# Spreading w_out's block sums, two banks for the last pass, and copies ahead of activations in a feed-forward kernel

## The chip, the cores and the metric

One core of a Trainium2 chip runs the whole program. The metric is device time in microseconds for one execution, and lower is better. TensorE does the matmuls; VectorE and ScalarE read its banks, split numbers into a high and a low part and do the elementwise work; GpSimd (POOL) scales attention operands; SyncE (SP) issues nearly all transfers.

## The reference

Linear attention with a decay for each head (4 sequences, 8 heads, 768 positions of 64) gives x, which goes through a feed-forward layer:

```
attn_out = _attn_ref(q, k, v, lam)                 # 4 x 8 x 768 x 64
x = attn_out.transpose(0, 2, 1, 3).reshape(3072, 512)
h = x @ w_in                                       # 3072 x 2048
r = np.maximum(h, 0.0)
out = (r * r) @ w_out                              # 3072 x 512
```

All of it is in fp32. The matmuls take each factor as a high part and a low part and add three products: high by high, high by low, low by high.

## The kernel before, in words

The 3072 tokens are six slices (m = 0 to 5) of 512 tokens, that is, of four chunks of 128. The hidden features are 16 blocks of 128 (f = 0 to 15), or 8 pairs.

Slices 0 and 1 go straight: for each f, 12 matmuls of 128x512 for `x @ w_in`, then relu and square, then `project`, 12 matmuls into four accumulator banks. The other four are done two and two by a block scheme with 7 products where 8 would be needed. The loop over `pair(0, i, ...)` makes the hidden features of slices 2 and 3: for each pair of f, 7 products of 6 matmuls (`product`, banks X, Y, Z), joined by VectorE's adds into `temp`, and beside it the projection of slice 2 and the attention of slices 4 and 5. Then the fourth slice (m2 = 3) is projected: `again` casts the kept features `r` to a high part `gh` on ScalarE and a low part `gl` on VectorE, two buffers each, and `project` follows one step behind. Between these steps stand sums and parts of x (`x_sums`, `x_parts`) for the last two slices. The loop over `NPAIR` at line 1305 is the last w_in phase: the 7 products of each pair for slices 4 and 5, features kept in `k1`, `k2`, `l1`, `l2`, on which `kept` does relu and square in place. Its last pair begins to prepare the w_out stage (`prepare`: a cast to the high part on ScalarE, a subtraction for the low part on VectorE). Last comes `whole(0)` and `whole(1)`: the same scheme for `@ w_out`, seven passes of 48 matmuls of 128x256 for each of the two slices, on banks X, Y and Z.

Four of those passes need w_out's blocks added and subtracted. For each of the 8 units u (the blocks u and u + 8), `t_sums` does two adds and four subtractions on VectorE and a cast on ScalarE, `t_parts` the low part on VectorE, and `t_store` sends both parts to DRAM, from where `t_fetch` brings them into a ring of slots in the last stage. Units 0 to 5 (`SUMMED`) are done in the first six pairs of slices 2 and 3, units 6 and 7 in steps 2, 4 and 8, 10 of the fourth slice's projection.

Every engine runs its instructions in the order in which the program writes them; nothing reorders them. SyncE's transfers too wait in their order. A weight of the pairs is fetched 8 products ahead (`RING`), at the end of a product.

Of the kernel before, what the change touches and what calls it, by code (L numbers as in the profile page):

```python
# [7 lines left out]
F32 = mybir.dt.float32  # L8
F32R = mybir.dt.float32r
# [3 lines left out]
ALU = mybir.AluOpType  # L13
PSUM = bass.MemoryType.PSUM

P = 128
# [6 lines left out]
DM = H * D  # L23
# [3 lines left out]
G = 4  # L27
# [8 lines left out]
NPAIR = NF // 2  # L36
RING = 8
EARLY = 2 * NF - 3
SUMMED = 6
SUMS = (1, 2, 3, 5, 6, 7, 9, 11)  # L40
HALF = DM // 2

# [2 lines left out]
def body(ctx: ExitStack, tc: tile.TileContext, qT, kT, kvq, lam, w, out):  # L45
    nc = tc.nc
# [3 lines left out]
    wk = ctx.enter_context(tc.tile_pool(name="wk", bufs=2))  # L50
# [5 lines left out]
    V = nc.vector  # L56
# [156 lines left out]
    raw, cv, hole, beside, third = {}, {}, None, [], []  # L213
# [100 lines left out]
    Z = T - 1  # L314
# [8 lines left out]
    x = ZP  # L323
# [12 lines left out]
    for k in range(4):  # L336
# [394 lines left out]

    T1, T3, T4, T2 = range(4)

    def t_sums(u, sums):
        x = sums[:, 0]
        for k in range(2):
            j = w_out(u + k * NPAIR)
            add(
                x[:, 2 * k : 2 * k + 2].rearrange("p a n -> p (a n)"),
                wh[:, j].bitcast(F32), wl[:, j].bitcast(F32),  # L740
            )
        b11, b12, b21, b22 = (x[:, k] for k in range(4))
        sub(b11, b12, b11)
        sub(b12, b22, b12)
        sub(b22, b22, b11)
        sub(b21, b21, b22)
        nc.scalar.copy(sums[:, 1].bitcast(F32R), x)

    def t_parts(sums):
        x = sums[:, 0]  # L750
        V.tensor_tensor(out=x.bitcast(F32R), in0=x, in1=sums[:, 1], op=ALU.subtract)

    def t_store(u, sums):
        for k in range(2):
            nc.sync.dma_start(out=td[u, :, :, k], in_=sums[:, 1 - k])
# [75 lines left out]
    def kept(r):  # L831
        nc.scalar.activation(r, r, AF.Relu)
        nc.scalar.activation(r, r, AF.Square)
# [263 lines left out]
    for i in range(NPAIR):  # L1097
        t = (PLAIN + 2) * G + i

        def attention(first, then):  # L1100
            more = i + 1 < NPAIR
            x = burst(t + 1, True, more, first)
            then()
            keep(t, x)
            if i < SUMMED:
                t_parts(sums)
            if more:
                masked(t + 1)
                state(t + 1)
                prep_q(t + 1)  # L1110
                copy_vx(t + 1)
                copy_qx(t + 1)
            if i + 2 < NPAIR:
                load_kq(t + 2)
                load_v(t + 2)
                prep_k(t + 2)

        def between():
            nonlocal sums
            project(*p)  # L1120
            if i == 0:
                sums = wk.tile([P, 2, 4, HALF], F32, name="sums", tag="raw")
            if i < SUMMED:
                t_sums(i, sums)

        p = prev
        pair(0, i, temp, between, attention)
        if i < SUMMED:
            t_store(i, sums)
        prev = (m1, 2 * i + 1)  # L1130
    sums = sets[0].bitcast(F32).rearrange("p (k a n) -> p k a n", k=2, a=4)
    again(m2, 0)
# [1 line left out]
    for f in range(NF):  # L1134
        if f + 1 < NF:
            again(m2, f + 1)
        if f % 2 and f < 14:
            x_sums(f // 2)
            x_parts(f // 2)
        if f in (2, 8):  # L1140
            t_sums(SUMMED + f // 6, sums)
        if f in (4, 10):
            t_parts(sums)
            t_store(SUMMED + f // 6, sums)
        if f + 1 < NF:
            project(m2, f)
    prev = (m2, NF - 1)
# [87 lines left out]
    def multiply(n, j, bank, i, begin, end):  # L1235
        s_, p, k = n // 14, n // 2 % 7, n % 2
        w_, _ = factor(p, s_, k * G + j)
        at = j % 2 * HALF + i * C
        h, l = (part(n, e)[:, j // 2, at : at + C] for e in range(2))
        o = bank[:, i * HALF : (i + 1) * HALF]  # L1240
        for q, (x, y) in enumerate(((h, 0), (h, 1), (l, 0))):
            nc.tensor.matmul(  # L1242
                o, x, w_[:, y], start=begin and i == 0 and q == 0, stop=end and q == 2,
                skip_group_check=True,
            )

# [9 lines left out]
    def whole(s_):  # L1256
        p1, u2, u3, c11 = (temp[:, k] for k in range(4))
        banks_ = {}
        for p in range(7):
            if p in (0, 1, 4):  # L1260
                banks_["XY..Z"[p]] = ps_acc.tile([P, DM], F32, name="acc")
            bank = banks_["XYXYZYZ"[p]]
            begin, last = p in (0, 1, 4), p == 6 and s_ == 1
            for k in range(2):
                n = s_ * 14 + p * 2 + k
                prepare(n + LEAD)
                if last:
                    continue
                for j in range(G):
                    for i in range(2):  # L1270
                        multiply(n, j, bank, i, begin and k == 0 and j == 0, k == 1 and j == G - 1)
                    e = factor(p, s_, k * G + j)[1]
                    if e is not None:
                        t_fetch(e + len(t_ring))
            if p == 0:
                nc.scalar.copy(p1, bank)
            elif p == 1:
                nc.scalar.copy(u2, bank)
            elif p == 2:
                nc.scalar.copy(c11, bank)  # L1280
                send(s_, 0, 0, c11)
            elif p == 3:
                add(u3, bank, p1)
                sub(u2, u3, u2)
            elif p == 4:
                add(u3, bank, u3)
                send(s_, 1, 1, u3)
            elif p == 5:
                add(p1, bank, p1)
                send(s_, 1, 0, p1)  # L1290
            elif not last:
                add(u2, bank, u2)
                send(s_, 0, 1, u2)
            else:
                for i in range(2):
                    for k in range(2):
                        for j in range(G):
                            multiply(s_ * 14 + p * 2 + k, j, bank, i, False, k == 1 and j == G - 1)
                    cs = slice(i * HALF, (i + 1) * HALF)
                    add(u2[:, cs], bank[:, cs], u2[:, cs])  # L1300
                    t = (PLAIN + 3) * G + i
                    nc.sync.dma_start(out=out[t * C : (t + 1) * C, HALF:DM], in_=u2[:, cs])

    place = [r_of[k] for k in range(G)]
    for i in range(NPAIR):
        n = (NPAIR + i) * 7
        f1, f2 = 2 * i, 2 * i + 1
        p1, u2, u3, _ = (temp[:, k] for k in range(4))
        k1, k2 = (g_place(0, f) for f in (f1, f2))
        l1, l2 = (g_place(1, f) for f in (f1, f2))  # L1310
        X = ps_h.tile([P, N], F32, name="h")
        product(n, X, True)
        nc.scalar.copy(p1, X)
        Y = ps_h.tile([P, N], F32, name="h")
        product(n + 1, Y, True)
        add(u2, Y, p1)
        if i == NPAIR - 1:
            prepare(0)
        if i in range(1, 5):
            for s_ in range(2):  # L1320
                x = g_kept[s_][(i - 1) // 2][0][:, (i - 1) % 2 * 2 : (i - 1) % 2 * 2 + 2]
                sub(x[:, :, HALF:DM], x[:, :, 0:HALF], x[:, :, HALF:DM])
        product(n + 2, X, False)
        nc.scalar.activation(X, X, AF.Relu)
        nc.scalar.activation(k1, X, AF.Square)
        product(n + 3, Y, False)
        if i == 0:
            project(*prev, place=place)
        add(u3, Y, p1)
        Z = ps_acc.tile([P, N], F32, name="acc")  # L1330
        product(n + 4, Z, True)
        add(l2, Z, u3)
        product(n + 5, Y, False)
        add(k2, Y, p1)
        kept(l2)
        if i == NPAIR - 1:
            prepare(1)
        product(n + 6, Z, False)
        add(l1, Z, u2)
        kept(k2)  # L1340
        kept(l1)
    for n in range(2, LEAD):
        prepare(n)
    for n in range(len(t_ring)):
# [56 lines left out]
```

## Time and profile before

| | us |
|---|---|
| median of three runs | 584.71 |
| lowest, highest | 584.45, 585.79 |
| the profiled execution, its own time | 585.68 |
| its span, first to last instruction | 583.9 |
| TensorE busy with matmuls | 569.7 (98%) |
| TensorE busy with weight loads | 477.2 (82%) |
| VectorE busy | 390.0 (67%) |
| ScalarE busy | 337.1 (58%) |
| GpSimd busy | 84.4 (14%) |

A matmul's time in a row includes its latency, and rows of neighbours overlap, so "busy 98%" says that TensorE is rarely empty, not that it is never held up. Where it is held up shows in what the weight loads (PEld) and the matmuls (PE) waited for, and in the distance from one matmul's start to the next. The stages follow each other in time: opening and slices 0 and 1 until 232 us, the pairs of slices 2 and 3 until 371, the projection of the fourth slice until 419, the last w_in phase until 499, the w_out stage until the end.

### The profile page before, as it was taken

Reading aid. Unit: us, or ns where it says so; the run is one execution under the profiler, and the core shown is the slowest. Engines: PE = TensorE matmul, PEld = TensorE weight load, DVE = VectorE, ACT = ScalarE, POOL = GpSimd, SP = SyncE. Lnnn points to the kernel's source line nnn. Section 1 sums busy time; section 2 is a strip of 40 time slices with the busy share of each in tenths; the row PEclk is TensorE's granted clock in tenths of the full one; section 3 lists DMA queues with packets and bytes.
Section 4 is the critical chain, followed back from the end, with each engine's and each line's share of the span. In section 5 each row is a group of like instructions: output and inputs, shape, how many; then the busy total and the mean of one; then the engine's idle time right before and its main releaser. Section 6 shows DMA issues by size and latency. Waiting matters only on the chain.

```text
span 583.9 us, 13621 instructions
## 1 busy us (share of the span) xinstructions
PE 569.7 (98%) x5519; PEld 477.2 (82%) x5519; DVE 390.0 (67%) x687; ACT 337.1 (58%) x597; POOL 84.4 (14%) x96
## 2 busy tenths in 40 slices
PE   7899999999999999899999999998999999999997
PEld 5777888888888888788888888876878787999997
DVE  5899999936868676665677643467544434786771
ACT  3799989845656655555655545544356565643440
POOL 6512422332223100011111111000000000000000
PEclk7799999999999999999999999999999999999999
DMA  8668667145998853778666773321277664899431
GB/s 317 215 238 279 223 218 239 45 149 200 322 345 299 309 177 104 235 235 267 201 204 203 261 238 107 127 73 36 62 225 186 196 188 121 289 342 359 143 112 54
DMA packets 70270, 118.85 MB, mean 204 GB/s; under 512 B 5952, under 2 KB 31040, under 8 KB 70208
## 3 DMA queue, kind: packets, MB, share of 16 engines
q1 hardware_dynamic: 70208, 117.99, 61.2%
q8 instruction: 43, 0.70, 0.5%
q14 instruction: 19, 0.16, 0.1%
HBM read 88.60 MB, written 29.36 MB: 202 GB/s over the span
## 4 chain that ended last, share of the span: by engine, by line
PE 92%; DVE 3%; DMA 2%; issue 1%; ACT 1%; SPq 0%; POOL 0%; DVEq 0%; POOLq 0%
PE h L805 22%; PE h L637 15%; PE acc L1242 14%; PE acc L673 10%; PE acc L678 9%; PE acc L674 9%; PE h L433 4%; PE acc L805 4%; PE b L433 2%; PE att L433 2%; DMA set<-in_kvq 1%; DVE set L347 1%; DMA set<-in_w 1%; PE open L433 1%; DVE sums L347 1%
## 5 line engine op out<-in xcount | busy, mean ns | idle before, releaser
L673 PE MATMUL acc<-w,gh 128*128 128x512 f32 x224 | 89.7, 400 | 1.8 <-ACT gh L837 1.8
L678 PE MATMUL acc<-w,gl 128*128 128x512 f32 x224 | 87.7, 391 | 0.2 <-DVE gl L658 0.2
L674 PE MATMUL acc<-w,gh 128*128 128x512 f32 x224 | 87.5, 391 | 0.0
L805 PE MATMUL h<-w,ring 128*128 128x512 f32 x288 | 70.5, 393 | 1.6 <-DVE r L347 1.6
L805 PEld LDWEIGHTS h<-w,ring 128*128 128x128 f32 x288 | 53.4, 188 | 14.9 <-DVE r L347 2.3
L658 DVE TENSOR_TENSOR gl<-h,gh 128x512 fp32r<-128x512 f32 x40 | 27.5, 688 | 53.6 <-ACT h L653 53.6
L1242 PE MATMUL acc<-w 128*128 128x256 f32 x492 | 60.9, 283 | 0.5 <-DVE temp L347 0.5
L1242 PEld LDWEIGHTS acc<-w 128*128 128x128 f32 x492 | 59.9, 192 | 0.8 <-DVE temp L347 0.7
L637 PE MATMUL h<-xh,w 128*128 128x512 f32 x240 | 60.1, 392 | 0.0
L644 ACT ACTIVATE h<-h 128x512 f32<-128x512 f32 x40 | 23.3, 583 | 60.7 <-PE h L637 44.0
L347 DVE TENSOR_TENSOR temp<-h,temp 128x512 f32<-128x512 f32 x40 | 27.5, 689 | 41.8 <-PE h L805 33.1
L637 PEld LDWEIGHTS h<-xh,w 128*128 128x128 f32 x240 | 44.7, 188 | 10.0 <-DVE w L295 0.4
L673 PEld LDWEIGHTS acc<-w,gh 128*128 128x128 f32 x224 | 42.0, 188 | 12.4 <-ACT gh L837 3.1
L505 POOL TENSOR_TENSOR qs<-set,qpow 128x512 f32<-128x512 f32 (+1 forms) x21 | 26.4, 1255 | 174.5 <-PE b L433 172.9
L678 PEld LDWEIGHTS acc<-w,gl 128*128 128x128 f32 x224 | 42.0, 188 | 10.3 <-DVE gl L658 1.4
L674 PEld LDWEIGHTS acc<-w,gh 128*128 128x128 f32 x224 | 42.1, 188 | 8.6 <-POOL w L298 0.4
L805 PE MATMUL h<-w,wz 128*128 128x512 f32 x144 | 35.8, 393 | 0.0
L805 PE MATMUL h<-w 128*128 128x512 f32 x144 | 35.7, 392 | 0.0
L1220 DVE TENSOR_TENSOR w<-kept,w 128x1024 fp32r<-128x1024 f32 (+2 forms) x32 | 25.2, 820 | 10.9 <-ACT w L1219 10.9
L637 PE MATMUL h<-xl,w 128*128 128x512 f32 x120 | 32.2, 390 | 0.1
L1219 ACT CAST w<-kept 128x1024 fp32r<-128x1024 f32 (+2 forms) x32 | 22.6, 727 | 16.5 <-PE acc L1242 15.8
L805 PEld LDWEIGHTS h<-w,wz 128*128 128x128 f32 x144 | 26.7, 188 | 6.5 <-ACT temp L848 0.3
(240 smaller groups left out, 1168.6 us busy)
## 6 DMA issues: line engine op xcount, KB each, us to landing
ring<-wd SPq DMA_DIRECT2D x56, 256.0 KB, 3.1
raw<-in_w SPq DMA_DIRECT2D x22, 512.0 KB, 5.0
w<-td SPq DMA_DIRECT2D x42, 256.0 KB, 5.3
set<-in_kvq SPq DMA_DIRECT2D x16, 512.0 KB, 3.9
wd<-hl SPq DMA_DIRECT2D x16, 512.0 KB, 5.0
w<-wd SPq DMA_DIRECT2D x28, 256.0 KB, 3.0
wz<-wd SPq DMA_DIRECT2D x28, 256.0 KB, 2.9
td<-sums SPq DMA_DIRECT2D x12, 512.0 KB, 5.4
```

Source lines behind the costliest of these rows:

```text
L347: lambda o, x, y, op=op: V.tensor_tensor(out=o, in0=x, in1=y, op=op)
L433: nc.tensor.matmul(self.banks[row][rows[col], at : at + D], lhsT, rhs, start=key not in self.begun, stop=stop, skip_group_check=True,)
L505: nc.gpsimd.tensor_tensor(out=z, in0=x, in1=w_, op=ALU.mult)
L637: nc.tensor.matmul(h, wt[:, w_in(f), kt * P : (kt + 1) * P], x[:, kt], start=k == 0, stop=k == 11)
L644: nc.scalar.activation(h, h, AF.Relu)
L658: V.tensor_tensor(out=gl, in0=r, in1=gh.bitcast(F32), op=ALU.subtract)
L673: nc.tensor.matmul(accs[m][i], gh[:, cs], wh[:, j], start=f == 0, stop=False)
L674: nc.tensor.matmul(accs[m][i], gh[:, cs], wl[:, j], start=False, stop=False)
L678: nc.tensor.matmul(accs[m][i], gl[:, cs], wh[:, j], start=False, stop=end)
L805: nc.tensor.matmul(bank, w[:, kw * HALF + kt * P : kw * HALF + (kt + 1) * P], x_slot(2 * c + kt, kx), start=first and q == 0, stop=q == 5, ...
L1220: V.tensor_tensor(out=l, in0=x, in1=h.bitcast(F32), op=ALU.subtract)
L1242: nc.tensor.matmul(o, x, w_[:, y], start=begin and i == 0 and q == 0, stop=end and q == 2, skip_group_check=True,)
```

## The change

- `t_sums` is cut in three: `t_whole` (the two adds), `t_sums` (the four subtractions, or some of them) and `t_high` (the cast). `t_parts` is now `t_low`.
- The first pair of slices 2 and 3 carries no sums. The next five pairs carry units 0 to 4.
- Units 5 and 6 stand in the fourth slice's projection: adds at steps 0 and 6, subtractions at 2 and at 8 and 10, casts at 3 and 11, low parts and stores at 4 and 12.
- Unit 7 stands in the first three pairs of the last w_in phase.
- There, `kept(k2)` and `kept(l1)` move from a pair's end to the next pair, behind the copy of its first bank X.
- In the second slice of the last stage, bank Z's two halves of 256 columns lie in two banks (Z and z) in passes 4 and 6; the add of pass 4 is done half by half.

```
-SUMMED = 6
+SUMMED = 5
...
-            if i < SUMMED:
-                t_sums(i, sums)
+            if 0 < i <= SUMMED:
+                t_whole(i - 1, sums)
+                t_sums(sums)
+                t_high(sums)
...
-        if f in (2, 8):
-            t_sums(SUMMED + f // 6, sums)
-        if f in (4, 10):
-            t_parts(sums)
-            t_store(SUMMED + f // 6, sums)
+        if f in (0, 6):
+            t_whole(SUMMED + f // 6, sums)
+        if f in (2, 8, 10):
+            t_sums(sums, {2: (0, 1, 2, 3), 8: (0, 1), 10: (2, 3)}[f])
+        if f in (3, 11):
+            t_high(sums)
+        if f in (4, 12):
+            t_low(sums)
+            t_store(SUMMED + f // 12, sums)
...
-                o, x, w_[:, y], start=begin and i == 0 and q == 0, stop=end and q == 2,
+                o, x, w_[:, y], start=begin and q == 0, stop=end and q == 2,
...
+            if p == 4 and s_ == 1:
+                banks_["z"] = ps_acc.tile([P, DM], F32, name="acc")
             bank = banks_["XYXYZYZ"[p]]
+            pair_ = (bank, banks_["z"]) if "z" in banks_ and bank is banks_["Z"] else (bank, bank)
...
-                    add(u2[:, cs], bank[:, cs], u2[:, cs])
+                    add(u2[:, cs], pair_[i][:, cs], u2[:, cs])
...
         nc.scalar.copy(p1, X)
+        for x in remaining:
+            kept(x)
+        if i == 2:
+            t_high(sums)
         Y = ps_h.tile([P, N], F32, name="h")
         product(n + 1, Y, True)
         add(u2, Y, p1)
+        if i == 0:
+            t_whole(U, sums)
         if i == NPAIR - 1:
             prepare(0)
...
         add(l2, Z, u3)
+        kept(l2)
         product(n + 5, Y, False)
         add(k2, Y, p1)
-        kept(l2)
         if i == NPAIR - 1:
             prepare(1)
         product(n + 6, Z, False)
         add(l1, Z, u2)
-        kept(k2)
-        kept(l1)
+        if i < 2:
+            t_sums(sums, (2 * i, 2 * i + 1))
+        elif i == 2:
+            t_low(sums)
+            t_store(U, sums)
+        remaining = [k2, l1]
+    for x in remaining:
+        kept(x)
```

VectorE in the first pair of slices 2 and 3, before (`o` are the drain copies of slice 1, `r` the add that frees bank Z):

```order
L347 TENSOR_TENSOR temp<-h,temp 128x512
L682 COPY o<-acc 128x512 x2
L347 TENSOR_TENSOR sums<-w 128x512 x2
L347 TENSOR_TENSOR sums<-sums 128x256 x4
L347 TENSOR_TENSOR r<-h,temp 128x512
```

The same place after:

```order
L347 TENSOR_TENSOR temp<-h,temp 128x512
L682 COPY o<-acc 128x512 x2
L347 TENSOR_TENSOR r<-h,temp 128x512
L347 TENSOR_TENSOR temp<-h,temp 128x512
L347 TENSOR_TENSOR r<-h,temp 128x512
```

The six instructions of the sums are gone from between the drain copies and the adds.

ScalarE in the fourth slice's projection, before, from step 8's sums on (`set_94` holds the sums, `gh` are the high parts, `w<-held` the casts of x's sums):

```order
L747 CAST set_94<-set_94 128x1024
L837 CAST gh<-r 128x512
L780 CAST w<-held_1638 128x512 x2
L837 CAST gh<-r 128x512 x2
L780 CAST w<-held_1638 128x512 x2
L837 CAST gh<-r 128x512 x2
```

The same place after:

```order
L840 CAST gh<-r 128x512 x2
L783 CAST w<-held_1638 128x512 x2
L840 CAST gh<-r 128x512 x2
L783 CAST w<-held_1638 128x512 x2
L750 CAST set_94<-set_94 128x1024
L840 CAST gh<-r 128x512 x2
```

The cast of the sums has moved behind the next two pairs of casts of x's sums, that of step 11, and stands ahead of the high part that `again(m2, 13)` casts.

ScalarE at the start of the last pair of the last w_in phase, before (`temp<-h` is the copy of bank X, `w<-set_94` the cast of the w_out stage):

```order
L832 ACTIVATE kept<-kept 128x512
L833 ACTIVATE kept<-kept 128x512
L832 ACTIVATE kept<-kept 128x512
L833 ACTIVATE kept<-kept 128x512
L1313 COPY temp<-h 128x512
L1219 CAST w<-set_94 128x2x512
L1324 ACTIVATE h<-h 128x512
```

The same place after:

```order
L1337 COPY temp<-h 128x512
L835 ACTIVATE kept<-kept 128x512
L836 ACTIVATE kept<-kept 128x512
L835 ACTIVATE kept<-kept 128x512
L836 ACTIVATE kept<-kept 128x512
L1228 CAST w<-set_94 128x2x512
L1354 ACTIVATE h<-h 128x512
```

The four activations have moved from ahead of the copy to between the copy and the cast. VectorE's order is the same there before and after: the add to `temp`, the cast's low part (`w<-set_94,w`), the next add to `temp`.

## Rows read from the trace of the kernel before

**Rows 1.** The page's slices of the span: granted clock of TensorE, in tenths

```profile
PEclk7799999999999999999999999999999999999999
```

**Rows 2.** What weight loads waited for: us in total, times, longest

```profile
PEld acc L673 <- ACT gh L837: 3.1, 3, 1.7
...
PEld h L805 <- ACT temp L1313: 2.0, 7, 0.3
...
PEld acc L678 <- DVE gl L658: 1.4, 3, 0.6
```

**Rows 3.** Order of time, first pair: start, us, engine, line, operation [idle before]

```profile
240.55 2.88 PE L805 MATMUL h<-w,ring 128*128 128x512 f32 x12
...
241.36 1.28 DVE L347 TENSOR_TENSOR sums<-w 128x512 f32<-128x512 f32 x2
...
242.56 1.79 DVE L347 TENSOR_TENSOR sums<-sums 128x256 f32<-128x256 f32 x4
...
245.01 1.66 PE L805 MATMUL h<-w,ring 128*128 128x512 f32 x6 [1.58 <-DVE r L347]
```

**Rows 4.** Fourth slice's fifteen projections: window, us, busy by engine, clock, DMA share, GB/s

```profile
374.15:418.73 44.58, 42.58 (x182) 33.25 (x180) 31.67 (x48) 18.33 (x32) 0.00 (x0) 1.00 0.19 68
```

**Rows 5.** Order of time, VectorE and ScalarE, around unit 6's sums

```profile
382.04 1.79 DVE L347 TENSOR_TENSOR set<-set 128x256 f32<-128x256 f32 x4
...
383.87 1.05 ACT L747 CAST set<-set 128x1024 fp32r<-128x1024 f32 x1 [3.68 <-DVE set L347]
384.82 0.61 ACT L837 CAST gh<-set 128x512 fp32r<-128x512 f32 x1
...
385.47 0.69 DVE L658 TENSOR_TENSOR gl<-set,gh 128x512 fp32r<-128x512 f32 x1 [1.63 <-ACT gh L837]
```

**Rows 6.** Order of time there: the low part, then a step with sums of x

```profile
387.88 1.22 DVE L751 TENSOR_TENSOR set<-set 128x1024 fp32r<-128x1024 f32 x1
...
394.05 0.62 ACT L837 CAST gh<-r 128x512 fp32r<-128x512 f32 x1 [2.10 <-PE acc L674]
...
397.61 0.62 ACT L837 CAST gh<-r 128x512 fp32r<-128x512 f32 x1
```

**Rows 7.** Order of time, start of the third pair of the last w_in phase

```profile
440.97 2.88 PE L805 MATMUL h<-w,ring 128*128 128x512 f32 x12
...
442.56 0.63 ACT L833 ACTIVATE set<-set 128x512 f32<-128x512 f32 x1
443.09 0.57 ACT L1313 COPY temp<-h 128x512 f32<-128x512 f32 x1
...
443.71 3.03 PE L805 MATMUL h<-w 128*128 128x512 f32 x12
444.30 0.69 DVE L347 TENSOR_TENSOR temp<-h,temp 128x512 f32<-128x512 f32 x1 [2.44 <-PE h L805]
```

**Rows 8.** Order of time, last pair of that phase: cast, low part, next add

```profile
492.00 1.05 ACT L1219 CAST w<-set 128x1024 fp32r<-128x1024 f32 x1
...
493.08 1.23 DVE L1220 TENSOR_TENSOR w<-set,w 128x1024 fp32r<-128x1024 f32 x1
...
495.21 0.69 DVE L347 TENSOR_TENSOR temp<-h,temp 128x512 f32<-128x512 f32 x1 [0.91 <-PE h L805]
```

**Rows 9.** Order of time, the last pass, its two halves

```profile
573.95 2.32 PE L1242 MATMUL acc<-w 128*128 128x256 f32 x18
...
577.03 0.42 DVE L347 TENSOR_TENSOR temp<-acc,temp 128x256 f32<-128x256 f32 x1 [2.18 <-PE acc L1242]
...
577.51 2.42 PE L1242 MATMUL acc<-w 128*128 128x256 f32 x18 [0.52 <-DVE temp L347]
```

**Rows 10.** The page's DMA issues: size, median us from issue to landing

```profile
w<-wd SPq DMA_DIRECT2D x28, 256.0 KB, 3.0
...
td<-sums SPq DMA_DIRECT2D x12, 512.0 KB, 5.4
...
td<-set SPq DMA_DIRECT2D x4, 512.0 KB, 3.0
```

More of the change, by code (lines that the diff above doesn't have):

```diff
@@ L732, in body, with t_whole @@
     T1, T3, T4, T2 = range(4)
-    def t_sums(u, sums):
+    def t_whole(u, sums):
         x = sums[:, 0]
@@ L741, in t_sums, with t_high, t_low @@
             )
[L742 to L751, printed above, removed]
+    def t_sums(sums, steps=range(4)):
+        b11, b12, b21, b22 = (sums[:, 0, k] for k in range(4))
+        order = (b11, b12, b11), (b12, b22, b12), (b22, b22, b11), (b21, b21, b22)
+        for k in steps:
+            sub(*order[k])
+    def t_high(sums):
+        nc.scalar.copy(sums[:, 1].bitcast(F32R), sums[:, 0])
+    def t_low(sums, cs=slice(0, 4)):
+        x = sums[:, 0, cs]
+        V.tensor_tensor(out=x.bitcast(F32R), in0=x, in1=sums[:, 1, cs], op=ALU.subtract)
     def t_store(u, sums):
@@ L1122, in between @@
                 sums = wk.tile([P, 2, 4, HALF], F32, name="sums", tag="raw")
-            if i < SUMMED:
-                t_sums(i, sums)
+            if 0 < i <= SUMMED:
+                t_whole(i - 1, sums)
+                t_sums(sums)
+                t_high(sums)
         p = prev
         pair(0, i, temp, between, attention)
-        if i < SUMMED:
-            t_store(i, sums)
+        if 0 < i <= SUMMED:
+            t_store(i - 1, sums)
         prev = (m1, 2 * i + 1)
@@ L1139, in body @@
             x_parts(f // 2)
-        if f in (2, 8):
-            t_sums(SUMMED + f // 6, sums)
-        if f in (4, 10):
-            t_parts(sums)
-            t_store(SUMMED + f // 6, sums)
+        if f in (0, 6):
[7 more added lines that the diff above has]
+            t_store(SUMMED + f // 12, sums)
         if f + 1 < NF:
@@ L1270, in whole @@
                     for i in range(2):
-                        multiply(n, j, bank, i, begin and k == 0 and j == 0, k == 1 and j == G - 1)
+                        multiply(
+                            n, j, pair_[i], i,
+                            begin and k == 0 and j == 0 and (i == 0 or pair_[1] is not bank),
+                            k == 1 and j == G - 1,
+                        )
                     e = factor(p, s_, k * G + j)[1]
@@ L1285, in whole @@
             elif p == 4:
-                add(u3, bank, u3)
+                for i in range(2):
+                    cs = slice(i * HALF, (i + 1) * HALF)
+                    if bank is pair_[1]:
+                        cs = slice(0, DM)
+                    if i == 0 or bank is not pair_[1]:
+                        add(u3[:, cs], pair_[i][:, cs], u3[:, cs])
                 send(s_, 1, 1, u3)
@@ L1297, in whole @@
                         for j in range(G):
-                            multiply(s_ * 14 + p * 2 + k, j, bank, i, False, k == 1 and j == G - 1)
+                            multiply(s_ * 14 + p * 2 + k, j, pair_[i], i, False, k == 1 and j == G - 1)
                     cs = slice(i * HALF, (i + 1) * HALF)
-                    add(u2[:, cs], bank[:, cs], u2[:, cs])
+                    add(u2[:, cs], pair_[i][:, cs], u2[:, cs])
                     t = (PLAIN + 3) * G + i
@@ L1304, in body @@
     place = [r_of[k] for k in range(G)]
+    sums = wk.tile([P, 2, 4, HALF], F32, name="sums", tag="raw")
+    U = NPAIR - 1
+    remaining = []
     for i in range(NPAIR):
@@ L1339, in body @@
         add(l1, Z, u2)
-        kept(k2)
-        kept(l1)
+        if i < 2:
+            t_sums(sums, (2 * i, 2 * i + 1))
+        elif i == 2:
+            t_low(sums)
+            t_store(U, sums)
+        remaining = [k2, l1]
+    for x in remaining:
+        kept(x)
     for n in range(2, LEAD):
```

## The prediction, made before the changed kernel ran

> **What bounds the kernel now.** I read the page's first two parts, then what the weight loads waited for, stage by stage, then the order of time around each wait. From the third slice of the page on TensorE is never long without work: its clock row stands at 9 (full) in all but the first two slices [rows 1], and a product of 128x512 starts every 0.227 us (12 of them in 2.72 us: 440.97 to 443.69 by [rows 7], where the row of 2.88 us is 11 steps and one latency of 0.39). So only what holds up TensorE's stream counts, and the matmuls themselves are not changed in number. The stream is held up at four places that this change touches: the first pair (once), the projection of the fourth slice (three times before a high part, three times before a low part [rows 2]), the start of seven pairs of the last w_in phase [rows 2], and the last bank [rows 9]. VectorE and ScalarE are far from full, but both take their work strictly in the order written, so a short sum waits where it stands and holds what stands behind it.
>
> **First pair of the third slice: gain 1.9.** Four drain copies and then six instructions of unit 0's sums (1.28 and 1.79 us) stand on VectorE ahead of the add that frees bank Z [rows 3]. The second six products should start 12 x 0.227 = 2.72 us after 240.55, at 243.27; they start at 245.01 and their row is 1.66 long where six need 1.52. Lost: 1.74 + 0.14 = 1.88 us. After the change nothing of the sums stands in that pair (the order fence shows it); the add can run when its six products end, about 242.1, and is done by 242.8. Pairs 2 to 6 carry the same number of sums as before, in the same place, with other unit numbers, and I cost them at nothing.
>
> **Projection of the fourth slice: gain 3.8, and 0.2 given back.** Fifteen projections of 12 matmuls need 15 x 2.72 = 40.8 us; the stretch from the first one to the next w_in product lasts 44.58 [rows 4]. Lost: 3.78. [rows 5] show how: the four subtractions run until 383.83, the cast of the sums (383.87, 1.05 us) waits for them on ScalarE, and the next high part's cast, 384.82, stands behind it, so its weight load comes late. The low part, 0.65 behind the high one, is then late too. The second block of sums does the same, and the delayed casts of the input's sums pass it on once more: three waits for a high part, 3.1 us, and three for a low part, 1.4 [rows 2]. After the change the cast of the sums is issued one projection after the subtractions, so it waits for nothing. The rest I followed projection by projection, with T for the start of a projection and 2.72 a step. First block: the two adds run at T0+1.4 to 2.6, the four subtractions at T2+1.3 to 3.0, the cast at T3+1.5 to 2.6, just before the next high cast may start (T4, when its buffer is read out), the low part (1.22 us [rows 6]) at T4+1.3 to 2.5: nothing is late. Two queues are passed: SyncE's two stores, with 512 KB each, land about 3.0 us later [rows 10], at T4+5.5, and the next unit's adds, which overwrite the sums, stand at T6+1.3 = T4+6.7; that leaves 1.2 us. Second block: the subtractions in two halves of 0.9 us fit behind the low parts of projections 9 and 11. The tight place is projection 11. There ScalarE's chain from one high cast to the next is 3.56 us because the input's sums come first on VectorE (394.05 to 397.61 [rows 6]); now the sums' cast adds 0.95 to it (a cast of 1.05, of which 0.1 overlaps its successor). So high part 13 is cast at T11+4.5 and done at 5.1, where its weight load is due at T11+5.2; low part 13 starts 0.65 later, ends at T11+5.8 and is due at T11+5.7. I take 0.2 us of new stall; the bounds are 0 (the low part just makes it) and 0.6 (the longest wait for a low part now [rows 2]).
>
> **Last w_in phase, copies first: gain 1.2.** Every pair's first copy of bank X stands on ScalarE behind four activations of the pair before (the last one at 442.56); it runs at 443.09, though product 1 ended at 442.5, and the third product's weights wait 0.3 [rows 2]. TensorE loses 0.17 of it: 0.02 in the start (443.71 for 443.69) and 0.15 in the row (3.03 for 2.88) [rows 7]. Seven such pairs: 7 x 0.17 = 1.17 us. With the copy first it runs at 442.53 to 443.1, and the four activations follow. Their late end costs nothing in pairs 2 to 5: with S for a pair's start (440.97), and 0.63 and some 0.04 for each, they are done at S+4.7, the subtractions on VectorE that need them end at S+5.4, and the add behind those isn't possible before S+5.6. If this cover of 0.2 us is gone, each of four pairs could lose up to that. The sums of unit 7 are spread here too: two adds (1.3 us) in the first pair, while VectorE waits for the late projection; two subtractions (0.9) after the last add of pairs 1 and 2, where it idles 2.4 us [rows 7]; the cast in pair 3 behind the activations, S+4.6 to 5.7, delaying only the square of X, which nothing needs before the next pair; the low part after pair 3's last add. Nothing of it is late.
>
> **Last pair: loss 0.9.** This is the price I find. Only there a cast of 1.05 us for the w_out stage follows the copy on ScalarE (492.00), its low part on VectorE follows (493.08), and the add that frees bank Y stands behind that low part on VectorE (495.21) [rows 8]. Here S is 489.41 (440.97 and five pairs of 42 x 0.227 + 0.17). With the copy first, four activations get between copy and cast: the cast moves to S+4.6, ends at S+5.66, the low part runs S+5.7 to 6.9 (the next starts 1.14 behind it), the add S+6.83 to 7.52, and the sixth product, due at S+6.80, starts at S+7.57. With the 0.14 that such a stall adds in its row (as in the first pair): 0.91 us. Bounds: 0.6 if activations run a little closer, 1.2 if the add also meets a slow semaphore.
>
> **Last bank: gain 0.76.** The second half's first matmul waits for the add that reads the first half of the same bank (577.03, then 577.51) [rows 9]; without it, it would follow 24 x 0.121 us after the first half's start at 573.95, at 576.85: 0.66, and 0.10 in the row of 2.42 (18 matmuls of the first half took 2.32). The halves in two banks need no such wait. The add of an earlier pass becomes two of 0.42 instead of one of 0.69 on a VectorE that idles microseconds there: nothing.
>
> **Sum.** -1.88 - 3.78 + 0.2 - 1.17 + 0.91 - 0.76 = -6.48 us. Span 583.9 becomes 577.4; the profiled execution's own time of 585.68 (1.78 outside its span) becomes 579.2. It is 0.97 above the median of the runs, 584.71; from that median the forecast is 578.2. Nothing else is then late: the stream is whole but for stalls that stay (about 0.13 in each of five pairs with sums, 0.3 in the first pair of the last phase) and the opening.
>
> **A page that speaks against one part.** The slices' projections change the accumulator bank every three matmuls, and the granted clock is 1.00 throughout [rows 4]. The Trainium skill, "TensorE: Matmul & The Clock Gate", section "A second HAM failure mode: psum-queue depth-cycling", says that a kernel cycling its banks in every iteration idled so finely that its clock swung between the two levels. The trace disagrees for this kernel, by the clock of 1.00 just named. As a mechanism here it is rival D.
>
> **The rivals.** A: no loss in the last pair and none at projection 11, the sum without the two positive terms: 584.71 - 7.59 = 577.1. For: both rest on chains added from latencies of 0.03 to 0.06. Against: the order is fixed, and the last pair's add is 0.77 too late, more than the latencies can hold. B: a stall of the projection is moved, not removed: with the second block's cast at projection 11 and its low part at 12, the longest wait for a high part, 1.7 [rows 2], stays in place of the 0.2: 584.71 - 6.48 + 1.5 = 579.7. For: ScalarE has 0.1 us to spare there, and everything behind it is in order. Against: the chain that I followed is made of rows, and gives the high part in time. C, the other side: SyncE. After pair 3 it waits for unit 7's low part before it may issue the next weight fetch: 0.7 late, and two issues of 0.56 more, about 1.9. The fetched weights are used 7 products, 9.5 us, after their issue, and land in 3.0, or behind the stores in 5.4 [rows 10]: 7.3 of 9.5. It decides once the landing takes over 7.6, and eats the whole gain from 14.1; at 15.5 the time is 586.1. The same stores in the earlier pairs run without such a wait, so little speaks for it. D: the two banks of the last slice's fifth pass alternate every three matmuls and the clock falls to 1.2 GHz for its 48 matmuls: 48 x 0.12 = 5.8 lost, 584.0, no change.
>
> **How the numbers follow.** Forecast 0.62, A 0.14, B 0.18, C 0.03, D 0.03. The range takes in A at its end and B, with 0.3 for the spread of a median of three runs below and 0.5 above: 576.9 to 580.3. Within 0.2% (1.2 us, about what a measurement of this kernel can tell from no change) lies D and nothing else: faster 0.94, same 0.03, slower 0.03.
>
> **What would show it.** Right: no weight load waits for r in the first pair; the fifteen projections take 41.0 or less; pairs of the last phase 9.52 apart and not 9.69; one new wait of 0.7 to 1.0 in the last pair, before its sixth product, for VectorE's add to temp; no idle time between the halves of the last bank. Wrong: waits for gh or gl of over 0.5 at projections 12 to 14, a wait for set or kept in pairs 2 to 5, or a weight load of the last w_in phase that waits for a DMA.

## The result, and the profile of the changed kernel

| | before | changed kernel | changed kernel again | with four more moves (e8_all) |
|---|---|---|---|---|
| median, us | 584.58 | 578.62 | 576.52 | 574.56 |
| lowest, highest | 584.32, 585.79 | 576.79, 579.66 | 576.35, 577.10 | 574.39, 576.28 |
| ratio to before, 95% interval | | 0.9891 (0.9861 to 0.9920) | 0.9859 (0.9846 to 0.9873) | 0.9835 (0.9818 to 0.9852) |
| span of the profiled execution | 583.9 | 574.9 | 575.3 | 572.8 |

The change makes the kernel 1.1% faster. The forecast was 578.2 us, a ratio of 0.9889. The second comparison, made later beside its own runs of the kernel before (median 584.93), gave 0.9859; what is known of the difference stands at the end of this section.

The page of the changed kernel, its span and busy times:

```profile
span 574.9 us, 13628 instructions
PE 566.5 (99%) x5519; PEld 477.1 (83%) x5519; DVE 389.7 (68%) x688; ACT 335.8 (58%) x597; POOL 83.7 (15%) x96
```

As many matmuls as before and the same busy time on VectorE and ScalarE, to 1.3 us: nothing was taken away, the work only waits less. Where the 9.0 us between the two spans went shows when the span is cut at the same instructions in both traces (the spans are rounded to 0.1 us, so the last row is good to about 0.05).

| stretch, us | before | after | gain |
|---|---|---|---|
| opening and slices 0 and 1, to the first product of slices 2 and 3 | 232.22 | 229.88 | 2.34 |
| first pair | 19.25 | 17.38 | 1.87 |
| pairs 2 to 8 | 122.68 | 122.72 | -0.04 |
| fourth slice's fifteen projections | 44.58 | 40.97 | 3.61 |
| last w_in phase | 80.36 | 79.91 | 0.45 |
| w_out stage to the end | 84.81 | 84.04 | 0.77 |

The windows of the changed kernel from which the row of the first pair and the last three rows are taken (window, us, busy time and count of PE, PEld, DVE, ACT, POOL, granted clock, DMA share, GB/s), with the first 29.2 us ahead of them:

```profile
0.00:29.20 29.20, 24.63 (x591) 18.90 (x595) 23.77 (x76) 16.86 (x36) 16.57 (x34) 0.82 0.79 291
...
229.88:247.26 17.38, 17.38 (x179) 14.19 (x178) 9.86 (x18) 9.71 (x20) 1.69 (x2) 1.00 0.88 287
...
369.98:410.95 40.97, 40.97 (x181) 33.71 (x180) 31.47 (x48) 18.54 (x32) 0.00 (x0) 1.00 0.20 74
410.95:490.86 79.91, 79.48 (x350) 65.16 (x348) 38.69 (x58) 43.61 (x73) 0.00 (x0) 1.00 0.66 192
490.86:574.90 84.04, 80.79 (x673) 80.58 (x671) 54.42 (x72) 34.06 (x49) 0.00 (x0) 1.00 0.65 220
```

The same views of the kernel before, where [rows 4] doesn't have them:

```profile
0.00:29.20 29.20, 22.90 (x573) 18.59 (x574) 20.85 (x73) 15.54 (x34) 17.33 (x34) 0.77 0.73 266
...
232.22:251.47 19.25, 17.67 (x179) 14.11 (x178) 13.67 (x21) 10.78 (x21) 1.81 (x2) 1.00 0.78 253
...
418.73:499.09 80.36, 80.34 (x349) 64.69 (x348) 34.29 (x50) 43.79 (x72) 0.00 (x0) 1.00 0.63 177
499.09:583.90 84.81, 81.04 (x673) 80.62 (x671) 54.45 (x71) 34.35 (x49) 0.00 (x0) 1.00 0.64 217
```

In the stretch of the projections PE is now busy in all of 40.97 us, where it was 42.58 of 44.58 [rows 4]. That is 15 times 2.72 and 0.17.

The first row of the table is not the change's. The instructions of the opening are the same in both kernels, and three kernels below whose opening is that of before (e3_bank_only, e4_cast_later, e2_copies_only) reach the same point at 229.89, 230.20 and 230.38 us; the profiled execution of before was slow there (232.22), with a granted clock of 0.77 in its first 29.2 us, and 0.82 in the execution of after. Without it the change is worth 6.66 us (the other five rows), beside a forecast of 6.48. The medians say 5.96 in the first comparison and 8.41 in the second. The second comparison's trace of the changed kernel has the stages of the first to 0.05 us each (17.39, 40.99, 79.91, 84.03) and an opening of 230.33, so these two executions, with spans of 575.3 and 574.9, differ by 0.4 us alone. The other three of the first comparison have spans of 576.4 to 577.9 and were not traced, and of the kernel before only one execution was: where the two comparisons part is not shown. The opening is the stretch that varies most in the traces there are.

### The profile page after: what moved, and what is told of

It is laid out like the page before. It is cut to its first block, busy times and chain, and to the rows that moved or that the text cites. A ratio compares the mean times of both kernels' runs of the same rounds, so it can differ in the third digit from the quotient of the medians.

```text
span 574.9 us, 13628 instructions
## 1 busy us (share of the span) xinstructions
PE 566.5 (99%) x5519; PEld 477.1 (83%) x5519; DVE 389.7 (68%) x688; ACT 335.8 (58%) x597; POOL 83.7 (15%) x96
## 4 chain that ended last, share of the span: by engine, by line
PE 93%; DVE 3%; ACT 2%; issue 1%; POOL 0%; DMA 0%; POOLq 0%
PE h L808 22%; PE acc L1251 14%; PE h L637 13%; PE acc L673 10%; PE acc L674 10%; PE acc L678 10%; PE h L433 4%; PE acc L808 4%; PE b L433 2%; PE att L433 1%; PE open L433 1%; DVE A L273 1%; DVE A L279 0%; DVE s L347 0%; DVE A L266 0%
```

## The places of the prediction, in the trace of the changed kernel

What weight loads waited for in the changed kernel (us in total, times, longest), to be read beside [rows 2]. The 3.1 for gh and the 2.0 for the copy are no longer on the list; of the waits for gl one, of 0.3, is in the projection; the 0.8 for temp is the last pair's; the three for r are not in the first pair but in later pairs of slices 2 and 3, as they were before:

```profile
PEld h L808 <- DVE temp L347: 1.3, 2, 0.8
...
PEld h L808 <- DVE r L347: 0.8, 3, 0.3
...
PEld acc L678 <- DVE gl L658: 0.6, 2, 0.3
```

Order of time in the changed kernel (start, us, engine, line, operation, idle before and its releaser): the first pair, then the projection's second block of sums, the third pair of the last w_in phase, its last pair, and the last bank.

```profile
238.21 4.24 PE L808 MATMUL h<-w,ring 128*128 128x512 f32 x18
...
239.77 0.69 DVE L347 TENSOR_TENSOR r<-h,temp 128x512 f32<-128x512 f32 x1 [0.67 <-PE h L808]
...
402.44 1.14 ACT L783 CAST w<-held 128x512 fp32r<-128x512 f32 x2 [1.89 <-DVE held L347]
403.49 1.05 ACT L750 CAST set<-set 128x1024 fp32r<-128x1024 f32 x1
404.44 0.61 ACT L840 CAST gh<-r 128x512 fp32r<-128x512 f32 x1
...
405.09 0.69 DVE L658 TENSOR_TENSOR gl<-r,gh 128x512 fp32r<-128x512 f32 x1 [0.70 <-ACT gh L840]
...
405.83 0.19 PEld L678 LDWEIGHTS acc<-w,gl 128*128 128x128 f32 x1 [0.30 <-DVE gl L658]
...
433.03 2.88 PE L808 MATMUL h<-w,ring 128*128 128x512 f32 x12
...
434.59 0.59 ACT L1337 COPY temp<-h 128x512 f32<-128x512 f32 x1 [2.06 <-PE h L808]
...
435.75 2.88 PE L808 MATMUL h<-w 128*128 128x512 f32 x12
...
482.19 0.59 ACT L1337 COPY temp<-h 128x512 f32<-128x512 f32 x1 [2.06 <-PE h L808]
...
485.06 1.03 ACT L1228 CAST w<-set 128x1024 fp32r<-128x1024 f32 x1
...
486.13 1.23 DVE L1229 TENSOR_TENSOR w<-set,w 128x1024 fp32r<-128x1024 f32 x1 [1.83 <-ACT w L1228]
...
487.27 0.68 DVE L347 TENSOR_TENSOR temp<-h,temp 128x512 f32<-128x512 f32 x1
488.01 1.23 PEld L808 LDWEIGHTS h<-w,ring 128*128 128x128 f32 x6 [0.83 <-DVE temp L347]
488.01 1.65 PE L808 MATMUL h<-w,ring 128*128 128x512 f32 x6 [0.41 <-DVE temp L347]
...
565.73 2.32 PE L1251 MATMUL acc<-w 128*128 128x256 f32 x18
...
568.61 2.32 PE L1251 MATMUL acc<-w 128*128 128x256 f32 x18
...
568.81 0.42 DVE L347 TENSOR_TENSOR temp<-acc,temp 128x256 f32<-128x256 f32 x1 [2.19 <-PE acc L1251]
```

First pair: 18 matmuls stand in one row, 17 steps of 0.227 and one latency, where [rows 3] had 12, a gap and 6. Projection: the sums' cast at 403.49 follows on what is ahead of it without idle time, and the high part of step 13 begins 0.1 before its end; the low part is 0.30 late, the only such wait in the stage. Third pair: the copy runs at 434.59, as soon as its product ends, and the next 12 matmuls start 2.72 behind the first 12, with a row of 2.88 and not 3.03 [rows 7]. Last pair: the cast comes 2.87 us behind the copy's start, the low part follows the cast, the add follows the low part, and the sixth product waits for the add: the chain that the prediction drew. Last bank: the second half starts 2.88 us behind the first, without a wait, and the add that reads the first half (568.81) runs beside it, where the second half waited for it in [rows 9].

## The experiments

The theory, as the prediction has it: four independent terms, each a wait that stands on one engine, and one new loss in the last pair, because four activations got between the copy and the cast. The rivals to be told apart: that the last pair's new wait is due to unit 7's sums and not to the copies; that the projection's gain comes from VectorE's sums being spread and not from the cast being issued later; that the two banks slow a pass; and that SyncE is near its limit.

**e1_sums_only: the change without its copies and its second bank.**

```
         nc.scalar.copy(p1, X)
-        for x in remaining:
-            kept(x)
...
         add(l2, Z, u3)
-        kept(l2)
         product(n + 5, Y, False)
         add(k2, Y, p1)
+        kept(l2)
...
         add(l1, Z, u2)
+        kept(k2)
+        kept(l1)
...
-            if p == 4 and s_ == 1:
-                banks_["z"] = ps_acc.tile([P, DM], F32, name="acc")
```

> The changed kernel without its two other parts: the activations stand again ahead of the copies of bank X, and the last pass has one bank; w_out's sums are spread as in the change, unit 7 in the last w_in phase. Theory (three separate gains, one separate loss that comes from the copies): first pair 17.4 us and not 19.25, the fifteen projections 41.0 and not 44.6, but the last w_in phase 80.4 as before, with seven waits of 0.3 for the copy and no wait of a sixth product for an add to temp, and the last bank's wait of 0.7 back. In all 5.5 us less than before, a ratio of 0.9907. Rival (the last pair's new wait comes from unit 7's sums, which now stand in that phase): the wait of 0.8 for temp is there without copies first. Rival (the sums hide behind something else and the copies carry the gain): ratio over 0.995.

Measured: 578.91 us, ratio 0.9903 (0.9887 to 0.9920); first pair 17.38, projections 40.97, last w_in phase 80.38, w_out stage 84.82. The sums alone hold the first pair's and the projection's gain, and unit 7's sums cost the last phase nothing (80.38 beside 80.36). What weight loads waited for in this kernel from the last w_in phase on:

```profile
PEld h L808 <- ACT temp L1334: 2.0, 7, 0.3
PEld acc L1251 <- DVE temp L347: 0.7, 1, 0.7
PEld h L808 <- DVE temp L347: 0.4, 1, 0.4
```

The waits of before are all there, and the wait of 0.8 in the last pair isn't: it doesn't come from the sums.

**e2_copies_only: the kernel before with the copies ahead.**

```
         nc.scalar.copy(p1, X)
+        for x in remaining:
+            kept(x)
...
         add(l2, Z, u3)
+        kept(l2)
         product(n + 5, Y, False)
         add(k2, Y, p1)
-        kept(l2)
...
-        kept(k2)
-        kept(l1)
+        remaining = [k2, l1]
+    for x in remaining:
+        kept(x)
```

> The kernel before with copies first alone. Theory: the seven waits of 0.3 for the copy are gone (1.17 us), one wait of 0.8 for an add to temp comes in the last pair, before its sixth product (0.7 lost): the last w_in phase takes 79.9 us and not 80.36; first pair 19.25, projections 44.6 as before. Rival (the wait comes from unit 7's sums): no such wait, phase 79.2. Rival (the activations' late end holds VectorE's subtractions in pairs 2 to 5): waits for temp in these pairs too, phase 80.4 or more.

Measured: 583.54 us; last w_in phase 80.02, the other stages as before. Waits of weight loads from that phase on:

```profile
PEld h L805 <- DVE temp L347: 1.5, 3, 0.8
```

Its last pair in order of time:

```profile
492.11 1.23 DVE L1220 TENSOR_TENSOR w<-set,w 128x1024 fp32r<-128x1024 f32 x1 [1.83 <-ACT w L1219]
493.25 0.68 DVE L347 TENSOR_TENSOR temp<-h,temp 128x512 f32<-128x512 f32 x1
493.98 1.23 PEld L805 LDWEIGHTS h<-w,ring 128*128 128x128 f32 x6 [0.83 <-DVE temp L347]
```

The seven waits for the copy are gone and the wait of 0.83 is there, so the copies bring both. Of its three waits for temp two are known (0.4 in the first pair, 0.83 in the last). The third, 0.26 in the third pair, is an old delay that becomes visible: VectorE's first add to temp starts 0.45 behind the end of its product there, and 0.09 to 0.10 behind it in the other seven pairs. The kernel before has the same 0.45 in its third pair (444.30 in [rows 7], with the product's end at 443.85), but there the copy's wait already delays the product that needs the bank. In the changed kernel this add starts 0.11 behind. What holds it for those 0.35 us was not found. It costs e2_copies_only 0.11, which is why the phase took 80.02 and not 79.9.

**e3_bank_only: the kernel before with the second bank.**

```
+            if p == 4 and s_ == 1:
+                banks_["z"] = ps_acc.tile([P, DM], F32, name="acc")
...
+            pair_ = (bank, banks_["z"]) if "z" in banks_ and bank is banks_["Z"] else (bank, bank)
...
-                    add(u2[:, cs], bank[:, cs], u2[:, cs])
+                    add(u2[:, cs], pair_[i][:, cs], u2[:, cs])
```

> The kernel before with the two banks of the last slice alone. Theory: the wait of 0.7 between the halves of the last pass is gone; from the w_out stage's first matmul to the end 84.05 us and not 84.8; everything ahead of it as before. Rival (alternating banks slows TensorE): the 48 matmuls of the fifth pass of the last slice take more than 5.85 us, up to 11.6, and the granted clock there is under 1.00.

Measured: 582.82 us; w_out stage 84.01 beside 84.81, its clock 1.00, and no weight load of that stage waits for the add any more. The last w_in phase, which this kernel doesn't touch, took 80.60 and not 80.36. The 0.24 builds up in steps of 0.01 to 0.02 over most of the pairs and is no single wait; e4_cast_later, which leaves this phase alone too, has 80.38. So one execution can be off by that much in a stretch that was left alone.

**e4_cast_later: the kernel before with the sums' casts issued later in the projection, and nothing else spread.**

```
-        nc.scalar.copy(sums[:, 1].bitcast(F32R), x)
+
+    def t_high(sums):
+        nc.scalar.copy(sums[:, 1].bitcast(F32R), sums[:, 0])
...
-        if f in (4, 10):
+        if f in (3, 10):
+            t_high(sums)
+        if f in (4, 12):
             t_parts(sums)
-            t_store(SUMMED + f // 6, sums)
+            t_store(SUMMED + f // 12, sums)
```

> The kernel before with the casts of units 6 and 7 alone deferred: from steps 2 and 8 of the fourth slice's projection to steps 3 and 10, the second low part from step 10 to 12; all six VectorE instructions stay together in one step, and the units are the old ones. Theory (it takes both: ScalarE must not wait, and VectorE's chain must be short where x's sums follow): the first block's loss of 0.9 is gone, the second keeps 1.3 of its 2.9, as the six instructions delay x's sums and with them the high part after next: projections 42.2 us, against 44.6 before and 41.0 in the change. Rival (the cast's wait was all of it): 41.0. Rival (VectorE's time was all of it): 44 or more.

Measured: projections 41.92. What weight loads waited for in this stretch:

```profile
PEld acc L678 <- DVE gl L658: 0.8, 2, 0.6
PEld acc L673 <- ACT gh L839: 0.7, 1, 0.7
```

Issuing the cast later is 2.66 of the 3.61; the first block loses nothing more. The second block keeps 1.1 us, and there its two adds and four subtractions still stand in one piece at step 8 (396.12 to 399.11 on VectorE). The sum of x behind them comes late, ScalarE's casts of it wait for it, and the high part behind those is the one that a weight load waits 0.7 for:

```profile
399.63 1.22 DVE L347 TENSOR_TENSOR held<-held 128x1024 f32<-128x1024 f32 x1
...
400.88 1.14 ACT L782 CAST w<-held 128x512 fp32r<-128x512 f32 x2 [3.63 <-DVE held L347]
```

The change has the remaining 0.95. In the projection it differs from this kernel by spreading those six instructions and the first block's, and by issuing the second cast at step 11 and not 10; the two were not run apart, but here the cast of step 10 (402.45) stands behind the late high part (401.93), so it isn't what delays it.

**e6_cast_first: the changed kernel with the w_out stage's first cast ahead of the four activations in the last pair.** `prepare_high` and `prepare_low` are the two halves of `prepare`.

```
         nc.scalar.copy(p1, X)
+        if i == NPAIR - 1:
+            halves[0] = prepare_high(0)
         for x in remaining:
             kept(x)
...
         if i == NPAIR - 1:
-            prepare(0)
+            prepare_low(halves[0])
```

> The change with one instruction moved: in the last pair of the last w_in phase the w_out stage's first cast stands on ScalarE right behind the copy of bank X, ahead of the four activations. Theory (the cast behind the activations, and VectorE's add behind its low part, are the new loss): the wait of 0.8 for an add to temp is gone, the phase takes 79.2 us and not 79.9; the activations end 1.0 later, at 6.6 behind the pair's start, and nothing waits for them. Rival (the activations then come too late for the w_out stage): a weight load of its first passes waits for VectorE, and the gain is given back.

Measured: 576.04 us; last w_in phase 79.22, w_out stage 84.09. Its last pair:

```profile
482.73 1.05 ACT L1335 CAST w<-set 128x1024 fp32r<-128x1024 f32 x1
...
486.33 0.69 DVE L347 TENSOR_TENSOR temp<-h,temp 128x512 f32<-128x512 f32 x1 [0.84 <-PE h L808]
...
487.49 1.52 PE L808 MATMUL h<-w,ring 128*128 128x512 f32 x6
```

The cast is 2.39 us earlier, counted from the pair's start, the add waits for its product again and not for the low part, the sixth product starts 2.72 behind the fourth (484.77) and without a wait. The 0.69 gained stays gained: the next stage is as long as before. That closes the question of the last pair.

**e7_three_stores: the changed kernel with unit 7's sums stored three times** (the same values to the same place), a test of rival C, SyncE.

```
             t_low(sums)
-            t_store(U, sums)
+            for _ in range(3):
+                t_store(U, sums)
```

> The change with unit 7's two stores issued three times in the third pair of the last w_in phase, six transfers of 512 KB in SyncE's queue. It prices the cover that the prediction's slower case rests on. Theory (the weight fetches wait in SyncE's order and land behind the stores, with 2 to 4 us to spare as the change has it): 2.2 us more of issues and 2 MB more ahead of the next fetches use the cover up; TensorE's weight loads wait for a DMA, 1 to 4 us in pairs 4 and 5, and the phase takes 81 to 84 us. Rival (the stores share the engines with the fetches and hold nothing): no wait for a DMA, 79.9.

Measured: 583.57 us. SyncE's issues there, in order of time, with TensorE's row, and what the stores waited for (us in total, times, longest):

```profile
443.60 9.44 SPq L758 DMA_DIRECT2D td<-sums  x6
453.14 1.84 SPq L799 DMA_DIRECT2D ring<-wd  x3
...
458.87 2.52 PE L808 MATMUL h<-w,ring 128*128 128x512 f32 x6 [4.84 <-DMA ring<-wd]
```

```profile
SPq L758 <- DMA td<-sums: 5.1, 4, 2.5
```

The windows behind that row (busy by engine, then granted clock, DMA share, GB/s):

```profile
459.50:462.50 3.00, 3.00 (x9) 2.32 (x8) 1.01 (x2) 0.00 (x0) 0.00 (x0) 0.50 0.70 259
...
465.00:475.00 10.00, 10.00 (x46) 8.29 (x45) 3.94 (x6) 5.25 (x9) 0.00 (x0) 1.00 0.70 192
```

In the changed kernel, the two issues stand on SyncE thus:

```profile
443.16 1.97 SPq L758 DMA_DIRECT2D td<-sums  x2
...
445.22 1.93 SPq L799 DMA_DIRECT2D ring<-wd  x3
```

The mechanism of rival C exists, and the changed kernel isn't near it: its weights are issued 2.0 us behind the stores' start, and no matmul waits. The size was missed, by something that the edit itself brought in. An issue takes 0.51 to 0.53 us here, near the prediction's 0.56, so six would take 3.1. Most of the rest of the 9.44 is waiting: 5.1 us in which the last four stores stand until earlier ones have landed, and 0.8 for the low part, which the changed kernel has too. Each of the four writes the place that the store two before it wrote, and goes out when that one has landed: by the chain of waits the second store lands at 449.39 and the fourth is issued at 449.47, that one lands at 452.51 and the sixth is issued at 452.52. So this run doesn't price more stores to places of their own; it shows what late weights cost. They were issued 9.5 us behind the stores' start and landed 5.6 later, and TensorE stood for 5.0 us (its product was due 1.36 behind the one at 452.51). The rest of the loss is the clock: after that stand the granted clock was 0.50 from 459.5 to 462.5, the lower of its two levels (1.2 GHz), and six matmuls took 2.52 and not 1.52. Of the 6.7 us that the phase lost (86.6 us to the next stage, for 79.9), 5.0 are the stand, and 1.7 are two products that took 2.31 and 2.10 from start to start and not 1.36.

**e8_all: e6 with the remaining waits taken on.** `pair` calls what it gets last (`rest_of_sums`) as `freed()`. The second block's cast moves from step 11 to step 12; in the pairs of slices 2 and 3 the last of the four subtractions and the cast go behind the add that frees bank Z; in the first pair of the last phase the add comes ahead of the late projection.

```
-        if f in (3, 11):
+        if f in (3, 12):
             t_high(sums)
...
-                t_sums(sums)
+                t_sums(sums, range(3))
...
+        def rest_of_sums():
+            if 0 < i <= SUMMED:
+                t_sums(sums, (3,))
                 t_high(sums)
...
-        pair(0, i, temp, between, attention)
+        pair(0, i, temp, between, attention, rest_of_sums)
...
         add(r_of[f2], Z, u3)
+        freed()
...
         product(n + 3, Y, False)
+        add(u3, Y, p1)
         if i == 0:
             project(*prev, place=place)
-        add(u3, Y, p1)
```

> The change with four more moves: the cast of e6; unit 6's cast one step later in the projection, behind the high part of step 12; the add to temp ahead of the late projection in the last w_in phase's first pair; and in the five pairs with sums the last subtraction and the cast behind the add that frees bank Z. Theory, by the waits of the change's trace: 0.7, 0.2, 0.3 and 5 x 0.13, 1.8 us in all: projections 40.8 us, last w_in phase 78.9, no wait for r in the pairs, a median of 576.8 where the change has 578.6, a ratio of 0.986 to the kernel before. Rival (each move holds up something new): the stage lengths of the change, or more.

Measured: 574.56 us (574.39 to 576.28), ratio 0.9835 (0.9818 to 0.9852). Against the changed kernel that was timed beside it, 576.52 (576.35 to 577.10), it is 2.0 us faster. Its pairs 2 to 8 and last phase, and the only wait that is left in that phase:

```profile
246.85:368.90 122.05, 122.05 (x1275) 100.96 (x1274) 70.78 (x139) 68.06 (x132) 14.84 (x12) 1.00 0.61 195
...
409.70:488.73 79.03, 79.03 (x350) 65.24 (x348) 38.44 (x57) 43.34 (x73) 0.00 (x0) 1.00 0.66 194
...
434.80 0.69 DVE L347 TENSOR_TENSOR temp<-h,temp 128x512 f32<-128x512 f32 x1 [1.66 <-ACT set L836]
...
435.55 1.23 PEld L808 LDWEIGHTS h<-w 128*128 128x128 f32 x6 [0.27 <-DVE temp L347]
```

Pairs 2 to 8 gain 0.67, the projections run at 15 x 2.72 exactly (40.80), the last phase gains 0.88. That is 0.69 as in e6, 0.32 in the first pair, where no weight load waits any more, so the add's place was the cause of that wait, and 0.13 lost in the third pair: there the delay of e2_copies_only is back, the add starts 0.46 behind its product's end, and a weight load waits 0.27 for it. The profile names an activation as what the add waited for, but in the kernel before the same add is as late and no activation ends there. e5_change_again is the changed kernel itself, timed beside e8_all; its numbers stand in the section on the result. Its ratio of 0.9859 lies below the 0.989 that was expected, with the same stage lengths.

> The changed kernel once more, beside the version with the four moves and on the same chip. Theory: a ratio of 0.989 to the kernel before; the same stage lengths as in its first profile (17.4, 41.0, 79.9, 84.0 us), while the opening, to the first product, differs by up to 3 us from run to run without cause in the code. Rival (the opening's 2.3 us in the first profile come from the change): an opening of 229.9 again.

## Why the prediction held, step by step

| step | forecast, us | measured | in |
|---|---|---|---|
| first pair | -1.88 | -1.87 | after, e1 |
| projection, the new stall taken off | -3.58 | -3.61 | after, e1, e4 |
| last w_in phase, copies | -1.17 | -1.16 | after, less the last pair |
| last pair | +0.91 | +0.71 | after, e2, e6 |
| last bank | -0.76 | -0.77 | after, e3 |
| sum | -6.48 | -6.70, with pairs 2 to 8 -6.66 | stages |

- First pair and last bank: the row of before gave the gap and the 0.1 to 0.14 that a stall adds to the row behind it, and both came off whole. (Of the four drain copies that the prediction puts on VectorE two are there, the other two on ScalarE; the sum doesn't use them.) The 0.04 that pairs 2 to 8 lost with other unit numbers is nothing.
- Projection: the tight place was named right. High part 13 was cast at 404.44 and not, by the prediction's T11 + 4.5, at 404.40 (T11 is 399.90), its low part ended 0.08 behind T11 + 5.8, and the weight load was 0.30 late, inside the bounds of 0 and 0.6. TensorE lost 0.17 by it.
- Copies first: the pairs stand 9.52 apart (433.03 and 442.55), 0.17 less than before, and the cover of 0.2 us on VectorE held in all four pairs: no weight load waits for temp there. The 1.16 is the phase's 0.45 and the last pair's 0.71; e6, without the loss in the last pair, has a phase 1.14 shorter than before. That the third pair gains as much as the others was luck in part: the prediction didn't see the late add there, which would have cost 0.1, and in the changed kernel that add isn't late.
- Last pair: the mechanism was right and its size 0.2 too large. Start to start, it lost 0.58 at the sixth product (488.01 for 480.63 + 6.80), and 0.13 in its row. The mis-sized term is the cast's place: forecast S + 4.6, measured S + 4.43 (S is 480.63), and all that follows is as much earlier. The prediction took 0.63 and some 0.04 for each of the four activations. They start at 482.68, 483.34, 483.88 and 484.53, the cast at 485.06: every second step is 0.53 or 0.54. [rows 7] has such a step (442.56, then 443.09). The low bound of 0.6 was nearer than the value.
- The forecast, 578.2, lies between the two medians, 578.62 and 576.52; they differ by more than any error in the sum, and the stages don't tell why. So it is the stages that bear the sum out, to 0.2 us, and how near the forecast is to either median is partly luck: the second one, beside its own runs of before, lies below the range (whose ends, by the prediction's own sums, are 576.8 and 580.2).
- Rival A (no loss in the last pair) is refuted by the wait of 0.83, rival B (a stall of 1.5 moved to projection 12) by the 40.97. Rival C is refuted for this kernel by SyncE's rows; e7 shows that a weight fetch held up on SyncE does stop TensorE, with two more pairs of stores that wait for each other's landing. Rival D asked for a pass at half the clock: the w_out stage's clock is 1.00 and its 672 matmuls run in one chain of 80.6 us, 0.12 each. So what the section of the Trainium skill that the prediction weighed ("TensorE: Matmul & The Clock Gate", "A second HAM failure mode: psum-queue depth-cycling") tells of isn't seen here, with banks that change every three matmuls in the projections and in the last slice's fifth pass, and no wait in that chain.

What stays open: what makes one add in the third pair of the last phase 0.35 us late in the kernel before, e2, e3, e4 and e8 and not in the changed kernel, and where the difference between the two comparisons lies.

## What to carry to other kernels

An instruction that waits costs its engine nothing while the engine is half idle, but it costs everything that stands behind it in order: issue a short step only when its inputs are already there, one loop step later if need be, and look which buffer the instruction behind it frees. When something is moved ahead, read what it lets slip between two links of another chain: here the copies gained 0.17 in each of seven pairs and gave 0.7 back in the one pair whose cast was the start of a chain over two engines. Such a chain can be added up from the rows of before to about 0.2 us, and the remedy (the cast ahead of the activations as well) can be read from the same sum.

## What the runs showed that was not expected

- Stores repeated on SyncE: six stores of 512 KB to two places took 9.44 us, though an issue takes 0.51 to 0.53. The last four stood 5.1 us in all until earlier stores had landed, and the weight fetches stood behind them in SyncE's order.
- One stand of TensorE of 4.84 us was followed by a granted clock of 0.50 (1.2 GHz) from 459.5 to 462.5, and by 1.00 from 465 to 475; the clock made a quarter of what the phase lost. The first pair of before, with a weight load's wait of 2.0 us, has a granted clock of 1.00 throughout.
- The opening, with the same instructions, took between 229.47 and 232.22 us in ten traces, which is more than any term of this change but the projection's.
